# A routed two-layer block on one core: which gathers may run ahead of the last writes of X, and where two weight steps stand

## The chip, the core and the metric

The kernel runs on one core of one Trainium2 chip. The metric is the time of one execution on the device in microseconds (us); less is better. TensorE (PE) multiplies, VectorE (DVE) and ScalarE (ACT) work on what it leaves, GpSimd (POOL) issues the indexed transfers, SyncE (SP) issues most weight loads.

## The reference, cut to what matters

```python
# retention attention -> x (4608 rows of 512), then two routed layers
def _moe_ref(x, w_skip, w_gate, w1, w2):          # the first one, "A"
    do_compute = x @ w_skip > 0
    ...
    for e in range(8):                            # argmax expert of each row
        h = np.maximum(xc[mask] @ w1[e], 0.0)
        y[mask] = gate_w[mask, None] * (h @ w2[e])
    out[do_compute] = xc + y

def _moe2_ref(x, w_gate, w1, w2):                 # the second one, "B"
    logits = x @ w_gate
    cap = N // E                                  # 576 rows for each expert
    for idx in np.argsort(-logits.flatten()):     # greedy, highest logit first
        ...
    for e in range(8):
        out[mask] = np.maximum(x[mask] @ w1[e], 0.0) @ w2[e]
```

Layer B assigns rows greedily under a cap, so its experts are found one after another: expert 0's list needs all the logits, expert i+1's list needs what expert i took.

## The kernel before, in words

Every fp32 product is made as three products of a high part and a low part (H·H, H·L, L·H). A weight chunk of 512 KB is loaded into one of five raw buffers (`wraw`), ACT copies it into a high part (`w_split`, line 253), and DVE subtracts to get the low part (`w_rest`, line 187). There are four chunks of w1 and four of w2 for each expert.

Attention comes first and leaves its rows in X in DRAM. Layer A runs over eight experts of up to 352 rows each, in tiles of 128, 128 and 96: it gathers rows of X, multiplies, and scatters the changed rows back into X. Layer B runs over eight experts of 576 rows (tiles of 128, 128, 128, 128 and 64): `gather` (line 637) takes the rows by the expert's list `ids2`, `turn` transposes them on PE and leaves `xTH` and `xTL`, `layer1` writes `l1p` in two segments of columns, 0:256 and 256:576, `layer2_half` (line 737, from the raw w2) multiplies the 64 remaining rows, `layer2` (line 710) the four full tiles. For expert 0, all eight blocks f of the segment 0:256 come before those of 256:576; for the others the segments alternate block by block. The results leave through ACT and DVE (`y`) and a scatter into the output.

The rows that layer A's last expert (7) writes can belong to expert 0's list, while that list should be known early. Its rows stand in columns NT to NT+2 of the routing tables (`NC = NT + 3` columns). `first_slots` (line 1206) gives the rows of the columns from `NL` on the last slots of expert 0's list, so that the first gathers need none of them. With `NL = NT + 1`, the tiles 1 and 2 of expert 7 (224 rows) are late, and the first two gathers are free of them. `post_a` (line 1087) therefore scatters expert 7's tile 0 as soon as it is done and holds back the scatters of tiles 1 and 2 (`held_x`) until `opening` (line 1444) has issued gathers 0 and 1. Gathers 2 to 4, and the low parts of w1's chunks 0 and 1, follow after the last products of layer A. Gathers wait for every earlier scatter into X, and scatters into X wait for every earlier gather.

A planner orders the work while the program is written: `tick` adds the columns of each matmul at 2400 per us to `clock`, and every generator in `tasks` goes on when its due time (the sum of what it yields, held to no more than 0.4 behind the clock) has come. Nothing of this runs on the chip: it fixes each engine's order of instructions, and the semaphores do the rest. The generators that matter here:

- `phases` (lines 1219 to 1398) makes the lists of layer B: five rounds of counting (`cnt`, `sum`, `nfl`), then the expert's number `eix`, the prefix sums (`pfx`, `slt`), the one-hot tables (`OHh`, `MV`, `OHl`), the product `idp` (line 1340), `pt`, `idq`, and the list `ids2`. The list of expert i+1 is made while expert i is multiplied, and the phase goes on to the next expert without waiting for the pass.
- `weights_b(i)` waits until expert i+1 is known, issues the load of its first w1 chunk on SP (the number is read from `eix`), yields 3.0, copies the chunk on ACT, yields 1.5, and makes its low part on DVE; the other loads follow.
- `rows_b(i)` gathers and turns the rows of expert i+1 after its list.

For expert 0, `entry` makes the low parts of chunks 2 and 3 and turns tiles 2 to 4 during the first segment; `task(gen)[1] = clock[0] + 4.5` lets the phases go on 4.5 planner us after layer A.

Of the kernel before, what the change touches and what calls it, by code (L numbers as in the profile page):

```python
# [21 lines left out]
N, DM, FF, E = 4608, 512, 1024, 8  # L22
NT = 36
# [24 lines left out]
MAGIC = 12582912.0  # L48
HL = 33.0 * (ZOFF - 1)
NC = NT + 3  # L50
NL = NT + 1
NQ = NC + 1
NG = NQ // 4
SPLIT = 26
# [116 lines left out]
def block_kernel(ctx, tc, q_c, k_c, k_r, v_r, wg, wg2, w1a, w2a, w2t, w1b, w2b, cst, dtab, out, dbg=None):  # L171
# [14 lines left out]
    def tt(o, x, y, op):  # L186
        V.tensor_tensor(o, x, y, op)  # L187

    def ts(o, x, s1, op0, s2=None, op1=None):
        if op1 is None:  # L190
            V.tensor_scalar(o, x, s1, None, op0)
        else:
            V.tensor_scalar(o, x, s1, s2, op0, op1)  # L193

    def stt(o, x, sc, y, op0, op1):
        V.scalar_tensor_tensor(o, x, sc, y, op0, op1)  # L196
# [48 lines left out]
    def w_split(kind, c, low="pool", over=False, swap=False):  # L245
        r = wt["whole", kind, c] = wt.pop(("raw", kind, c))
        if over:
            h, l = [rawp.tile([P, 1024], F32R, name=f"ov{c}", tag="wraw") for c in "HL"]
        else:
            tag = {"w1": "w2", "w2": "w1"}[kind] if swap else kind  # L250
            h = wp.tile([P, 1024], F32R, name=f"{kind}H{c}", tag=f"{tag}H{c}")
            l = wp.tile([P, 1024], F32R, name=f"{kind}L{c}", tag=f"{tag}L{c}")
        nc.scalar.activation(h, r, AF.Copy)  # L253
        wt[kind, c] = (h, l)
        if low != "later":
            e = nc.gpsimd if low == "pool" else V
            e.tensor_tensor(l, r, h.bitcast(F32), ALU.subtract)

    def w_rest(kind, c, half=None):
        h, l = wt[kind, c]  # L260
        j = slice(0, 1024) if half is None else slice(512 * half, 512 * half + 512)
        tt(l[:, j], wt["whole", kind, c][:, j], h[:, j].bitcast(F32), ALU.subtract)
# [114 lines left out]
    with ExitStack() as actx:  # L377
# [188 lines left out]
        gen = iter(())  # L566
        for i in range(-4, NT):
# [20 lines left out]
            if i == SPLIT + 2:  # L588
                gen = route(0, SPLIT, lambda: ps_1.tile([P, 512], F32, name="qc", tag="rt1"),
                            lambda: ps_1.tile([P, 48], F32, name="idp", tag="rt1"))  # L590
# [44 lines left out]
    def gather(key, i, ids, n, tag="xg", bufs=6):  # L635
        t = xp.tile([P, DM], F32, name="xg", tag=tag, bufs=bufs)
        nc.gpsimd.indirect_dma_start(out=t[0:n, :], out_offset=None, in_=X[:, :],  # L637
                                     in_offset=bass.IndirectOffsetOnAxis(ap=ids[0:n, :], axis=0))
        xg[key, i] = t
# [102 lines left out]
    def scatter(dst, idx, src, n):  # L742
        nc.gpsimd.indirect_dma_start(out=dst[:, :], out_offset=bass.IndirectOffsetOnAxis(ap=idx, axis=0),  # L743
                                     in_=src[0:n, :], in_offset=None)
# [33 lines left out]
    def gate_dots(x2, dst, n, a, b):  # L778
        for e in range(a, b):
            j = xp.tile([P, DM], F32, name="junk", tag="junk", bufs=1)  # L780
            V.scalar_tensor_tensor(j[0:n], x2[0:n], 1.0, wgb[e // 4][0:n, e % 4], ALU.mult, ALU.mult,  # L781
                                   accum_out=dst[0:n, e:e + 1])
# [298 lines left out]
    done_a = set()  # L1081

    def release():
        while held_x:
            held_x.pop(0)()

    def post_a(e, late=False):
        def post(i, n, p):
            j = 3 * e + i
            idx = ids1[0:n, j:j + 1]  # L1090
            x2 = xp.tile([P, DM], F32, name="x2", tag="x2", bufs=4)

            def whole():
                stt(x2[0:n], p[0:n], gate[0:n, j:j + 1], xg.pop((e, i))[0:n], ALU.mult, ALU.add)

            if late:
                def job():
                    whole()
                    if e == E - 1 and i and "open" not in done_a:
                        held_x.append(lambda: scatter(X, idx, x2, n))  # L1100
                    else:
                        scatter(X, idx, x2, n)
                    if e == E - 1 and i == 0:
                        done_a.add(0)

                fill.append(job)
                return
            if e < LATE:
                whole()
            else:  # L1110
                nc.scalar.activation(x2[0:n], p[0:n], AF.Copy, scale=gate[0:n, j:j + 1])
                nc.gpsimd.tensor_tensor(x2[0:n], x2[0:n], xg.pop((e, i))[0:n], ALU.add)
            scatter(X, idx, x2, n)
            if e < LATE:
                l8 = xp.tile([P, E], F32, name="l8", tag="l8", bufs=4)
                for c in range(0, E, 2):
                    pend.append(lambda c=c: gate_dots(x2, l8, n, c, c + 2))
                pend.append(lambda: scatter(LT, idx, l8, n))
        return post
# [86 lines left out]
    def first_slots(inc, rk2, s_, b_, slt, t2):  # L1206
        a, z_ = slice(0, NL), slice(NL, NC)
        every, early, tied = inc[:, 0, NC - 1:NC], inc[:, 0, NL - 1:NL], inc[:, 1, NL - 1:NL]
        ts(slt[:, a], rk2[:, 1, a], every, ALU.add, float(CAP2), ALU.is_ge)
        stt(slt[:, a], slt[:, a], 9999.0, rk2[:, 1, a], ALU.mult, ALU.add)  # L1210
        stt(slt[:, a], slt[:, a], early, b_[:, a], ALU.add, ALU.mult)
        stt(slt[:, z_], rk2[:, 1, z_], every, b_[:, z_], ALU.add, ALU.mult)
        cb = rt("cb", [P, 1])
        ts(cb, every, tied, ALU.add, float(CAP2), ALU.min)
        tt(cb, cb, every, ALU.subtract)
        tt(t2[:, a], rk2[:, 0, a], s_[:, a], ALU.mult)
        stt(t2[:, z_], rk2[:, 0, z_], cb, s_[:, z_], ALU.add, ALU.mult)
# [169 lines left out]
    know, listed = set(), set()  # L1387
# [13 lines left out]
    clock = [0.0]  # L1401
    tasks = []

    def task(g):
        t = [g, 0.0]
        tasks.append(t)
        return t
# [13 lines left out]
    def load_b(i, eng=nc.sync):  # L1421
        r = eng.value_load(eix[0:1, i:i + 1], min_val=0, max_val=E - 1)
        return loads_dyn(r, w1b, w2b, eng=eng)

    def gathers_b(i):
        return [lambda k=k: gather(("b", i), k, ids2[:, i, k:k + 1], T2[k]) for k in range(5)]

    def late():
        yield 1.0
        gate_h(1, 0, hh, 7)  # L1430
        for d in gate_slots(1, L2[:, NT:NC, :]):
            yield d
        for d in last_claims():
            yield d
        for d in phases():
            yield d

    gen = late()

    def chain():  # L1440
        while 0 not in listed:
            yield next(gen)

    def opening():
        while 0 not in know or LATE not in done_a:
            yield 0
        for j in load_b(0)[0][0:3]:
            j()
        yield 4.0
        for c in range(3):  # L1450
            w_split("w1", c, "later", swap=True)
            yield 1.1
        while 0 not in listed or 0 not in done_a:
            if 0 in listed and fill:
                fill.pop(0)()
            yield 0
        for j in gathers_b(0)[0:2]:
            j()
        done_a.add("open")
        release()  # L1460

    first = [task(chain()), task(opening())]
    late_layers[0](tick)
    done_a.add(LATE)
# [4 lines left out]
            pass  # L1469
    while fill:  # L1470
        fill.pop(0)()
    for j in gathers_b(0)[2:5]:
        j()
    w_rest("w1", 0)
    w_rest("w1", 1)
    warm(ps1, "l1", 16)
    t0 = turns(("b", 0), T2, (2, 3))
    t0[0]()
# [25 lines left out]
            open_t.pop(0)()  # L1504

    task(entry())
    task(gen)[1] = clock[0] + 4.5

    def post_b(i):
        def post(j, n, p):  # L1510
# [12 lines left out]
    def weights_b(i):  # L1523
        if i == 0:
            yield 15.0
        if held:
            for c in (2, 3):
                w_split("w1", c, "later", swap=True)
                yield 1.2
                w_rest("w1", c)  # L1530
                if c == 2:
                    held.pop()()
                yield 1.2
        for j in halves("w2", swap=True):
            j()
            yield 2.3
        if i + 1 == E:
            return
        while i + 1 not in know:
            yield 0  # L1540
        l1, l2 = load_b(i + 1)
        l1[0]()
        yield 3.0
        w_split("w1", 0, "later", swap=True)
        yield 1.5
        w_rest("w1", 0)
        while lay[0] < 2 * i + 1 or ("tail", i) not in done:
            yield 0
        for j in l1[1:]:
            j()  # L1550
        yield 2.3
        w_split("w1", 1, "later", swap=True)
        yield 2.3
        w_rest("w1", 1)
        for j in l2[0:3]:
            j()
        held.append(l2[3])
# [63 lines left out]
```

## Time and profile before

| | |
|---|---|
| median of three runs | 969.1 us (967.52 to 969.66) |
| the profiled execution: its time, its span | 972.4 us, 970.6 us |
| mean granted TensorE clock in it | 0.981 of full speed |
| busy in the span: PE, PE weight loads, DVE, ACT, POOL | 920.3, 772.1, 652.2, 318.7, 227.7 us |
| instructions: PE, DVE | 8288, 1679 |
| DMA moved | 153.92 MB, mean 159 GB/s |
| attention, layer A, layer B (from the span's start) | 0 to 186, 186 to 477, 477 to 971 us |

The page gives each engine's busy time, the chain of work that ended last, and the costliest groups of instructions with what ended the idle time ahead of them. In the trace, a row of the timeline is one instruction, or a few alike, with its start, its length, its engine and line, what it writes and reads, and in brackets the idle time of its engine ahead of it and what ended that. `L187`, `L193` and `L196` are the lines of helpers for DVE.

### The profile page before, as it was taken

How to read it: one execution, taken by the hardware profiler on the slowest of the kernel's cores; microseconds unless marked ns; L12 is line 12 of the kernel's file. 1: busy time of each engine (PE TensorE's matmuls, PEld its weight loads, DVE VectorE, ACT ScalarE, POOL GpSimd, SP SyncE). 2: the span in 40 equal slices, each digit the busy share in tenths (PEclk: the TensorE clock that was granted, in tenths of full speed). 3: DMA queues.
4: the chain of work that ended last, by engine and by line, in shares of the span. 5: the costliest groups of instructions: out<-in, count | busy, mean ns of one | idle time of the engine just before them, and what ended most of it. 6: DMA issues, size and time to landing. Idle time of an engine off the chain costs nothing.

```text
span 970.6 us, 20470 instructions
## 1 busy us (share of the span) xinstructions
PE 920.3 (95%) x8288; PEld 772.1 (80%) x8288; DVE 652.2 (67%) x1679; ACT 318.7 (33%) x607; POOL 227.7 (23%) x205
## 2 busy tenths in 40 slices
PE   7999998699999999999989999999999999999997
PEld 7888876598888888886676887968879789697885
DVE  3566576559999999968677767757667666664230
ACT  1333433133434334341232332423324233153330
POOL 1322221203354334320210304013030030330101
PEclk7999999799999999999999999999999999999999
DMA  9899996374454456330433406144061340633201
GB/s 333 327 401 353 342 356 216 121 248 140 159 194 150 157 173 190 118 134 12 138 123 104 168 5 224 44 140 132 1 228 45 126 134 14 222 121 115 87 6 43
DMA packets 46736, 153.92 MB, mean 159 GB/s; under 512 B 7248, under 2 KB 8016, under 8 KB 46384
## 3 DMA queue, kind: packets, MB, share of 16 engines
q1 hardware_dynamic: 31824, 106.98, 32.0%
q0 software_dynamic: 10496, 30.93, 9.6%
q10 hardware_dynamic: 4320, 14.68, 3.9%
q8 instruction: 66, 1.08, 0.5%
q14 instruction: 30, 0.25, 0.1%
HBM read 127.43 MB, written 25.13 MB: 157 GB/s over the span
## 4 chain that ended last, share of the span: by engine, by line
PE 57%; DVE 16%; issue 3%; DMA 3%; ACT 1%; POOLq 0%; SPq 0%; POOL 0%; DVEq 0%; ACTq 0%
PE l1p L679 27%; PE l2p L710 23%; DVE junk L781 5%; PE trp L660 2%; DMA wraw<-in_w1b_dram 2%; DVE w2L L187 2%; DVE hL L196 1%; DVE w1L L187 1%; PE l2p L737 1%; PE cnt L1250 1%; DVE xTL L187 1%; PE idp L1340 1%; DVE x L196 1%; DVE MV L187 1%; DMA xg<-X,ids 1%
## 5 line engine op out<-in xcount | busy, mean ns | idle before, releaser
L679 PE MATMUL l1p<-xTH,w1H 128*128 128x352 f32 (+2 forms) x768 | 242.4, 316 | 4.2 <-DVE hL L196 3.0
L679 PE MATMUL l1p<-xTL,w1H 128*128 128x352 f32 (+2 forms) x768 | 234.9, 306 | 1.6 <-DVE xTL L187 1.6
L679 PE MATMUL l1p<-xTH,w1L 128*128 128x352 f32 (+2 forms) x768 | 234.1, 305 | 0.0
L710 PE MATMUL l2p<-w2H,hH 128*128 128x512 f32 (+1 forms) x448 | 186.2, 416 | 0.0
L710 PE MATMUL l2p<-w2H,hL 128*128 128x512 f32 (+1 forms) x448 | 178.2, 398 | 0.0
L710 PE MATMUL l2p<-w2L,hH 128*128 128x512 f32 (+1 forms) x448 | 178.2, 398 | 0.0
L679 PEld LDWEIGHTS l1p<-xTH,w1H 128*128 128x128 f32 x768 | 145.5, 190 | 10.1 <-DVE hL L196 5.6
L679 PEld LDWEIGHTS l1p<-xTL,w1H 128*128 128x128 f32 x768 | 145.5, 189 | 2.8 <-DVE xTL L187 2.4
L679 PEld LDWEIGHTS l1p<-xTH,w1L 128*128 128x128 f32 x768 | 145.3, 189 | 0.0
L196 DVE SCALAR_TENSOR_TENSOR hL<-l1p,hH 128x256 fp32r<-128x256 f32 (+1 forms) x192 | 85.8, 454 | 77.9 <-ACT hH L688 77.4
L688 ACT ACTIVATE hH<-l1p 128x256 fp32r<-128x256 f32 (+1 forms) x192 | 78.6, 409 | 161.5 <-PE l1p L679 158.9
L743 POOL DMA_INDIRECT out_dram<-y,ids x40 | 42.0, 1050 | 374.6 <-DVE hm L193 141.0
L781 DVE SCALAR_TENSOR_TENSOR junk<-x,wgb 128x512 f32<-128x512 f32 (+1 forms) x144 | 99.0, 688 | 3.1
L710 PEld LDWEIGHTS l2p<-w2H,hL 128*128 128x128 f32 (+1 forms) x448 | 83.2, 186 | 21.7 <-issue 0.2
L710 PEld LDWEIGHTS l2p<-w2H,hH 128*128 128x128 f32 (+1 forms) x448 | 83.5, 186 | 18.8 <-issue 1.6
L710 PEld LDWEIGHTS l2p<-w2L,hH 128*128 128x128 f32 (+1 forms) x448 | 83.6, 187 | 16.9
L637 POOL DMA_INDIRECT xg<-X,ids x64 | 75.6, 1181 | 65.5 <-issue 28.7
L253 ACT ACTIVATE w1H<-wraw 128x1024 fp32r<-128x1024 f32 x64 | 65.4, 1056 | 70.8 <-DMA wraw<-in_w1b_dram 65.8
L661 ACT ACTIVATE xTH<-trp 128x512 fp32r<-128x512 f32 (+2 forms) x64 | 35.5, 558 | 124.9 <-PE trp L660 123.9
L187 DVE TENSOR_TENSOR w1L<-wraw,w1H 128x1024 fp32r<-128x1024 f32 x60 | 71.6, 1217 | 2.9 <-ACT w1H L253 2.5
L187 DVE TENSOR_TENSOR w2L<-wraw,w2H 128x1024 fp32r<-128x1024 f32 (+1 forms) x61 | 73.0, 1197 | 0.0
L253 ACT ACTIVATE w2H<-wraw 128x1024 fp32r<-128x1024 f32 x64 | 67.4, 1055 | 12.7 <-PE l2p L710 7.3
(263 smaller groups left out, 1127.4 us busy)
## 6 DMA issues: line engine op xcount, KB each, us to landing
wraw<-in_w2a_dram SPq DMA_DIRECT2D x31, 512.0 KB, 4.7
wraw<-in_w1b_dram SPq DMA_DIRECT2D x31, 512.0 KB, 4.6
wraw<-in_w1a_dram SPq DMA_DIRECT2D x28, 512.0 KB, 4.4
wraw<-in_w2b_dram SPq DMA_DIRECT2D x28, 512.0 KB, 4.2
X<-xo ACTq DMA_DIRECT2D x16, 512.0 KB, 6.7
kU<-in_k_c_dram SPq DMA_DIRECT2D x15, 512.0 KB, 9.1
qU<-in_q_c_dram SPq DMA_DIRECT2D x15, 512.0 KB, 7.7
vU<-in_v_r_dram SPq DMA_DIRECT2D x15, 512.0 KB, 8.4
```

What stands on the lines that cost most here:

```text
L187: V.tensor_tensor(o, x, y, op)
L196: V.scalar_tensor_tensor(o, x, sc, y, op0, op1)
L253: nc.scalar.activation(h, r, AF.Copy)
L637: nc.gpsimd.indirect_dma_start(out=t[0:n, :], out_offset=None, in_=X[:, :], in_offset=bass.IndirectOffsetOnAxis(ap=ids[0:n, :], axis=0))
L660: nc.tensor.transpose(p[:, k, 0:n], g[0:n, k * P:(k + 1) * P], ident[0:n, 0:n])
L661: nc.scalar.activation(h[:, :, off:off + n], p[:, :, 0:n], AF.Copy)
L679: nc.tensor.matmul(o, lhsT=wx[:, c:c + P], rhs=xx[:, k, a:b], start=(n == 0), stop=(n == 11))
L688: nc.scalar.activation(hh[0][:, f, a:b], o, AF.Relu)
L710: nc.tensor.matmul(p[0:n, :], lhsT=x[:, f, off:off + n], rhs=y[:, c:c + 512], start=(f == 0 and j == 0), stop=(f == 7 and j == 2))
L737: nc.tensor.matmul(p[64 * h:64 * h + 64, :], lhsT=ht[:, g], rhs=w[g // 2][:, c:c + 512], start=(f == 0), stop=(f == 3), tile_position=(0, ...
L743: nc.gpsimd.indirect_dma_start(out=dst[:, :], out_offset=bass.IndirectOffsetOnAxis(ap=idx, axis=0), in_=src[0:n, :], in_offset=None)
L781: V.scalar_tensor_tensor(j[0:n], x2[0:n], 1.0, wgb[e // 4][0:n, e % 4], ALU.mult, ALU.mult, accum_out=dst[0:n, e:e + 1])
```

## The change

Two columns instead of one are early (`NL = NT + 2`): only the 96 rows of expert 7's last tile take late slots. Expert 7's tile 1 is scattered as soon as it is done, tile 2 alone may be held, and `opening` waits for tile 1's job instead of tile 0's. Three gathers instead of two are then issued there, and the low parts of w1's chunks 0 and 1 are placed right behind them, no longer behind the last gathers. The phases go on 1.0 instead of 4.5 planner us after layer A. In `weights_b`, the planner time from the load of the next expert's first w1 chunk to its copy on ACT is 5.5 instead of 3.0.

```diff
-NL = NT + 1
+NL = NT + 2
@@ post_a
-                    if e == E - 1 and i and "open" not in done_a:
+                    if e == E - 1 and i == 2 and "open" not in done_a:
                         held_x.append(lambda: scatter(X, idx, x2, n))
                     else:
                         scatter(X, idx, x2, n)
-                    if e == E - 1 and i == 0:
-                        done_a.add(0)
+                    if e == E - 1 and i == 1:
+                        done_a.add(1)
@@ opening
-        while 0 not in listed or 0 not in done_a:
+        while 0 not in listed or 1 not in done_a:
             if 0 in listed and fill:
                 fill.pop(0)()
             yield 0
-        for j in gathers_b(0)[0:2]:
+        for j in gathers_b(0)[0:3]:
             j()
         done_a.add("open")
         release()
+        w_rest("w1", 0)
+        w_rest("w1", 1)
@@ after layer A
-    for j in gathers_b(0)[2:5]:
+    for j in gathers_b(0)[3:5]:
         j()
-    w_rest("w1", 0)
-    w_rest("w1", 1)
@@
-    task(gen)[1] = clock[0] + 4.5
+    task(gen)[1] = clock[0] + 1.0
@@ weights_b
         l1[0]()
-        yield 3.0
+        yield 5.5
         w_split("w1", 0, "later", swap=True)
```

## Rows read from the trace of the kernel before

**Rows 1.** PE's waits from 477 to 960 us: total, times, longest

```profile
PE idp L1340 <- DVE OHl L187: 12.1, 6, 2.3
```

**Rows 2.** Timeline of PE in pass 0, the list of expert 1

```profile
532.81 0.92 PE L1340 MATMUL idp<-MV,OHl 128*128 128x160 bf16 x10 [1.62 <-DVE OHl L187]
```

**Rows 3.** Timeline of pass 1 around the list of expert 2, engine by engine

```profile
577.73 0.18 PE L1262 MATMUL nfl<-fl,ones 128*128 128x8 bf16 x1
577.84 3.65 PE L737 MATMUL l2p<-wraw,hT 128*64 128x512 f32 x16
...
590.10 0.92 PE L1340 MATMUL idp<-MV,OHl 128*128 128x160 bf16 x10 [2.06 <-DVE OHl L187]
...
580.79 2.23 SPq L242 DMA_DIRECT2D wraw<-in_w1b_dram  x4
...
584.24 1.06 ACT L253 ACTIVATE w1H<-wraw 128x1024 fp32r<-128x1024 f32 x1 [5.82 <-DMA wraw<-in_w1b_dram]
585.20 0.57 ACT L1512 ACTIVATE y<-l2p 64x512 f32<-64x512 f32 x1
...
585.81 0.69 DVE L187 TENSOR_TENSOR y<-l2p,y 64x512 f32<-64x512 f32 x1 [2.75 <-ACT y L1512]
...
587.45 1.22 DVE L187 TENSOR_TENSOR w1L<-wraw,w1H 128x1024 fp32r<-128x1024 f32 x1
...
589.55 0.89 DVE L187 TENSOR_TENSOR OHl<-hl,kq 128x640 bf16<-128x640 bf16 x2
```

**Rows 4.** Windows, passes 1 and 2: length, five engines' busy (count), clock, DMA share, GB/s

```profile
549.60:610.30 60.70, 58.63 (x430) 49.16 (x429) 41.87 (x128) 20.11 (x42) 11.24 (x10) 1.00 0.33 109
610.30:672.40 62.10, 60.04 (x431) 49.96 (x429) 41.35 (x126) 20.31 (x42) 10.91 (x10) 0.97 0.32 107
```

**Rows 5.** Windows, columns of rows 4: one us of pass 2, three us after its stall

```profile
653.00:654.00 1.00, 1.00 (x4) 0.66 (x2) 0.36 (x1) 0.00 (x0) 1.00 (x1) 0.50 0.02 8
```

**Rows 6.** Timeline of PE in the opening of layer B

```profile
479.69 0.66 PE L660 MATMUL trp<-cs,xg 128*128 128x128 f32 x4 [0.64 <-DMA xg<-X,ids]
...
481.76 0.38 PE L679 MATMUL l1p<-xTL,w1H 128*128 128x256 f32 x1 [0.34 <-DVE xTL L187]
...
495.64 0.66 PE L660 MATMUL trp<-cs,xg 128*128 128x128 f32 x4 [2.05 <-DMA xg<-X,ids]
...
499.06 0.42 PE L679 MATMUL l1p<-xTL,w1H 128*128 128x320 f32 x1
...
503.24 0.41 PE L1250 MATMUL cnt<-OH,M 128*128 128x32 bf16 x10 [0.54 <-DVE M L187]
```

**Rows 7.** Timeline of POOL: scatters into X and gathers around the opening

```profile
456.46 0.99 POOL L743 DMA_INDIRECT X<-x,ids  x1 [21.25 <-DVE part L1252]
459.98 0.92 POOL L743 DMA_INDIRECT X<-x,ids  x1 [2.53 <-DVE fl L187]
...
476.00 0.97 POOL L637 DMA_INDIRECT xg<-X,ids  x1 [0.30 <-issue]
479.91 1.32 POOL L743 DMA_INDIRECT X<-x,ids  x1 [2.94 <-DMA xg<-X,ids]
484.61 1.51 POOL L743 DMA_INDIRECT X<-x,ids  x1 [3.38 <-DVE hL L196]
488.69 0.98 POOL L637 DMA_INDIRECT xg<-X,ids  x1 [2.58 <-issue]
```

**Rows 8.** Chain of waits: two blocks of layer 1 back to back (start, length)

```profile
617.50 3.27 PE l1p L679 x24
```

**Rows 9.** Timeline of DVE: tiles 1 and 2 of expert 7

```profile
471.72 0.75 DVE L196 SCALAR_TENSOR_TENSOR x<-l2p,gate,xg 128x512 f32<-128x512 f32 x1
...
477.36 0.75 DVE L196 SCALAR_TENSOR_TENSOR x<-l2p,gate,xg 96x512 f32<-96x512 f32 x1 [3.43 <-PE l2p L710]
```

**Rows 10.** Windows, columns of rows 4: the opening's first segment, and the counting after it

```profile
481.70:498.92 17.22, 13.47 (x109) 12.75 (x109) 11.30 (x41) 5.11 (x11) 4.37 (x4) 1.00 0.26 82
498.92:503.10 4.18, 3.78 (x25) 3.38 (x24) 3.97 (x11) 1.25 (x5) 0.00 (x0) 1.00 0.90 318
```

## The prediction, made before the changed kernel was run

> **What bounds the kernel now.** I read the page first: PE is busy for 95% of the span, so only idle PE and slow PE can be won. The waits of PE from the opening of layer B on come next: one line holds most of it, PE's list product `idp` waiting for DVE's one-hot table `OHl`, six times, 12.1 us [rows 1]. That is once in each of the passes 0 to 5 while the next expert's list is made: 1.62 in pass 0 [rows 2], about 2.1 in each of the passes 1 to 5, for which pass 1 stands.
>
> The timeline of pass 1 tells why [rows 3]. Call the start of the half product H (577.84). The last count matmul (`nfl`) stands just ahead of it, so the expert's number is known late and SP issues the load of its first w1 chunk at H+2.95. ACT's copy waits 5.82 us for that load, until H+6.40. The partial sum of the 64 rows stands behind the copy on ACT and gets out at H+7.36, though its product ended at H+3.65. DVE waits 2.75 us for it, and behind it come the rest of the list's tables and the low part of that chunk (1.22): `OHl` begins at H+11.7, and PE has stood still for 2.06 us. So a load that is asked for late and a copy that waits for it ahead of other work hold ACT, then DVE, then PE.
>
> The windows show a second price [rows 4]: pass 2 does the work of pass 1 in 62.1 instead of 60.7 us. Inside it the granted clock falls to 0.50 (1.2 GHz) after the stall [rows 5]. Passes 3 and 5 look like pass 2, pass 4 like pass 1: three falls, 1.4 us each.
>
> Last, the opening of layer B: there PE waits on gathers, 2.05 us in one place [rows 6], and the indexed transfers on X wait for one another [rows 7].
>
> **The change part by part.**
>
> *The copy and the phases.* They belong together. I add up the planner's yields by hand, before and after. The phases begin 3.5 planner us earlier and keep a lead of 2.8 to 3.5 through the passes 1 to 5. `nfl` and the number's load then stand 24 matmuls of layer 1 ahead of the half product, 3.3 us [rows 8]: the load is issued at H−0.3 instead of H+2.95. Its raw buffer is free (five tiles back is w1's chunk 3 of the running expert, split early in the pass), and SP has nothing else ahead of it. The copy, due 5.5 after the load, comes in the half product's third quarter: still ahead of the partial sum on ACT. But it now starts at about H+3.2 (load to copy took 3.45 [rows 3]) and ends at H+4.2, when the partial sum has been ready for only 0.6. That gets out at H+4.7, DVE adds it at H+4.8. On DVE the tables up to the first `MV` stand ahead of it; behind it come the second `MV` (0.5), the low part (1.1) and `OHl`: these begin at H+7.0, and `idp` can follow 0.55 later, the gap in [rows 3]: H+7.5. The planner puts `idp` 12 matmuls earlier than before, so PE has run dry at H+7.3 (before: 590.10 less 2.06, H+10.2; 27 matmuls from H+3.65 give 0.24 each). Left is 0.2 to 0.3 us of the 2.06: a gain of 1.8 in each of five passes, **9.0**. Bounds: 2.1 each if nothing is left (10.5); 1.3 each if the load takes half a us longer, or DVE is late by that (6.5).
>
> In pass 0 the copy comes after `idp` altogether; DVE has only the list's own tables, one low part of w2 (1.2) and the add of the partial sum ahead of it. I get `OHl` 0.2 after PE is ready: **1.4** of 1.62, bounds 1.0 and 1.6.
>
> *The clock.* With no stall of 2 us, the three falls should go: 3 × 1.4 = **4.2** in the profiled execution. Two executions need not have the same falls: passes 1 and 4 had the stall and no fall. For the median I take 1.4 to 4.2, middle 2.8.
>
> *The scatter of tile 1 ahead of the gathers.* This costs. Its x2 is made at 471.72 to 472.46 [rows 9], ahead of the list, so its scatter starts at 472.7. The gathers must now wait for its landing. From one transfer's start to that of the next dependent one the rows show 3.52 (456.46 to 459.98, a quiet moment), 4.70 and 4.08 [rows 7]; I take 4.1. So gather 0 starts at 476.8, and gather 1 at 478.1 instead of 476.00. The first layer-1 products start as much later, since they wait for tile 1's turn [rows 6]: **2.1 late** (1.5 to 2.7). The Trainium skill (DMA: Bandwidth & Descriptors, Anatomy of one DMA — SWDGE (gpsimd) path) gives such a transfer about 2.0 us and its bytes at 436 GB/s, an estimate of 2.6 us for 256 KB; by it gather 0 would start at 475.3 and the opening would be 1.5 better. The traces show none under 3.52 here.
>
> *Three gathers ahead, the low parts earlier.* Gather 2 goes out at about 479.4 instead of 488.69, gathers 3 and 4 behind the last scatter at about 487.5: none is waited for, and the 2.05 and the smaller wait ahead of it go. The two low parts (2.35 us) fill DVE's 3.43 us ahead of tile 2 [rows 9] and cost nothing there; they run while POOL waits for a landing.
>
> *What is late next.* DVE. Between the first full product (481.76) and the first product of the second segment (499.06 [rows 6]) lie 17.3 us, with 11.3 of DVE work [rows 10]. The earlier phases bring in the next expert's claims and first mask as well, nearly all of the 4.0 us that follow [rows 10], and the planner puts them ahead of the `xTL` of tile 4 that the second segment needs. That makes 15 of work, and about 16 with the gaps and DVE's wait for `cct`; the bank that each layer-1 block needs is freed by DVE behind this work. So the segment takes 16 instead of 17.3: 1.3 gained, not the 4 that PE alone would allow. After it, a wait of 0.54 for the first count [rows 6] is gone, and 0.15 of small matmuls come in. Opening: 2.1 − 1.3 − 0.4 = **0.4 slower**, from −0.5 to 1.2. And between 478 and 484 PE does little but turn two tiles: a fall of the clock, 1.4, is somewhat more likely than not there. With 0.9 for it, the opening costs **1.3** (−0.5 to 3.0).
>
> *The late slots* themselves change two columns instead of one in three small DVE instructions: nothing.
>
> **Sum.** 9.0 + 1.4 − 1.3 = 9.1 of stalls, and 2.8 of clock (4.2 in the profiled execution): 11.9. Against the profiled execution's own 972.4, with 4.2: 13.3, 959.1. The median, 969.1, is 3.3 below that execution, by the profiling or by two falls fewer; so from it I take 11.9: **957.2 us**.
>
> **The rivals.**
>
> 1. *The copy still holds DVE.* For it: it stays ahead of the partial sum, and `idp` comes earlier as well. Against: the load gains 3.3 us, the place of `idp` 2.9. If the chunk lands 1 us later than I take it, `OHl` does as well, half of each stall stays (5 lost) and the clock still falls (2.8 lost): 965.0.
> 2. *Slower: the load doesn't move.* Its mechanism is the load's start. If something besides the expert's number holds it to the half product (a raw buffer that this product still reads), the chunk lands no earlier against PE, the stall of 2.06 comes back whole at the new, earlier place, and the opening's price (1.3 to 3.0, and the 1.6 of pass 0 not won) is all that is left: 970.4 to 972.1. It decides from a landing later than H+5. Against it: by the order of the five raw buffers that chunk's is free long before, and SP has nothing else to wait for than the number.
> 3. *The gathers don't wait.* If the scatter lands within 2.6 us and DVE keeps up, the opening gains 3 instead of costing 1.3: 953.
> 4. *It doesn't do what it says.* The three gathers are issued ahead of X's last write, but wait for the last but one. That is in the forecast; alone it would leave the loop as forecast.
>
> **How the numbers follow.** Forecast 0.76 (952.5 to 962), rival 1 0.12, rival 2 0.07, rival 3 0.05. The range 952.0 to 963.5 runs from all stalls gone with three falls won and an opening that gains 0.5 (17 us) to 1.3 in each pass, one fall won and the opening at 3.0 (about 6 us); it leaves out rival 2 and most of rival 1. A measurement here tells about 0.2%, 2 us. Faster by more: forecast, rivals 1 and 3, less a little: 0.91. Within: the low end of rival 2: 0.04. Slower: 0.05.
>
> **What would show it.** In passes 1 to 5, the load's start against the half product (H−0.3), ACT's copy without a wait of 5.8, `idp` with an idle time under 0.5, and passes of about 58.5 us with a clock of 1.00. In the opening, a gather 0 that waits for a scatter until 476.8, no waits for gathers after tile 1, layer-1 blocks waiting for DVE, and a second segment that starts at 499 to 501. I would be wrong if the copy still waits long for its load, or if another engine's wait of 2 us stands in front of `idp`, `pfx` or the turns.

## The result, and the profile after

| | before | after |
|---|---|---|
| median | 969.4 us (967.5 to 975.5) | 958.5 us (956.5 to 960.5) |
| ratio after/before, 95% interval | | 0.988 (0.983 to 0.993) |
| the same on another chip, beside experiments | 970.0 us | 958.5 us, 0.9885 (0.986 to 0.991) |
| profiled execution: time, span, mean granted clock | 972.4, 970.6 us, 0.981 | 956.5, 954.8 us, 0.986 |

The median falls by 10.9 us, 1.1%, with an interval clear of 1; 957.2 was forecast. The waits of PE from 470 to 960 us come first (total, times, longest). The line of [rows 1] is gone, and the gathers and a count are what is left:

```profile
PE trp L660 <- DMA xg<-X,ids: 2.9, 2, 2.3
PE cnt L1250 <- DVE M L187: 2.2, 2, 1.2
```

Pass 1 again, engine by engine (start, length, engine, line, what it writes and reads, idle time ahead); these lines answer [rows 3]. H, the half product's start, is 576.17 here.

```profile
576.17 1.08 PE L737 MATMUL l2p<-wraw,hT 128*64 128x512 f32 x4
...
583.69 0.52 PE L1340 MATMUL idp<-MV,OHl 128*128 128x160 bf16 x5
...
575.86 4.65 SPq L242 DMA_DIRECT2D wraw<-in_w1b_dram  x4
...
579.15 1.06 ACT L253 ACTIVATE w1H<-wraw 128x1024 fp32r<-128x1024 f32 x1 [2.38 <-DMA wraw<-in_w1b_dram]
580.23 0.59 ACT L1512 ACTIVATE y<-l2p 64x512 f32<-64x512 f32 x1
...
580.85 0.69 DVE L187 TENSOR_TENSOR y<-l2p,y 64x512 f32<-64x512 f32 x1 [0.26 <-ACT y L1512]
...
581.95 1.22 DVE L187 TENSOR_TENSOR w1L<-wraw,w1H 128x1024 fp32r<-128x1024 f32 x1
583.08 0.88 DVE L187 TENSOR_TENSOR OHl<-hl,kq 128x640 bf16<-128x640 bf16 x2
```

The load starts at H−0.31, the copy at H+2.98, the table at H+6.91, and `idp` follows at H+7.52 with no idle time. ACT's order is the one of [rows 3]: the copy still stands directly ahead of the partial sum (579.15, then 580.23). The windows from one half product to the next, passes 1 and 2 (columns of [rows 4], which they answer), show equal lengths, PE busy throughout, and the clock at 1.00:

```profile
576.17:634.89 58.72, 58.72 (x429) 48.82 (x428) 41.41 (x125) 20.54 (x42) 12.51 (x10) 1.00 0.32 113
634.89:693.62 58.73, 58.73 (x429) 48.80 (x428) 41.39 (x125) 20.44 (x42) 12.49 (x10) 1.00 0.33 113
```

The opening of layer B has paid for this. First PE (answers [rows 6]), then POOL (answers [rows 7]), DVE around the x of tile 2 (answers [rows 9]), and two windows (columns of [rows 4]):

```profile
477.98 0.66 PE L660 MATMUL trp<-cs,xg 128*128 128x128 f32 x4 [2.29 <-DMA xg<-X,ids]
...
479.43 0.66 PE L660 MATMUL trp<-cs,xg 128*128 128x128 f32 x4 [0.57 <-DMA xg<-X,ids]
...
481.49 0.58 PE L679 MATMUL l1p<-xTL,w1H 128*128 128x256 f32 x1 [0.34 <-DVE xTL L187]
...
498.20 0.41 PE L1250 MATMUL cnt<-OH,M 128*128 128x32 bf16 x10 [1.19 <-DVE M L187]
498.47 0.39 PE L679 MATMUL l1p<-xTH,w1H 128*128 128x320 f32 x1
```

```profile
470.90 0.96 POOL L743 DMA_INDIRECT X<-x,ids  x1 [5.90 <-DVE pt L1343]
474.58 1.00 POOL L637 DMA_INDIRECT xg<-X,ids  x1 [2.72 <-DMA X<-x,ids]
475.88 0.98 POOL L637 DMA_INDIRECT xg<-X,ids  x1 [0.30 <-PE idle L232]
477.17 0.95 POOL L637 DMA_INDIRECT xg<-X,ids  x1 [0.31 <-issue]
481.72 0.93 POOL L743 DMA_INDIRECT X<-x,ids  x1 [3.61 <-DVE zd L1359]
```

```profile
471.37 2.36 DVE L187 TENSOR_TENSOR w1L<-wraw,w1H 128x1024 fp32r<-128x1024 f32 x2
474.81 0.74 DVE L196 SCALAR_TENSOR_TENSOR x<-l2p,gate,xg 96x512 f32<-96x512 f32 x1 [1.08 <-PE l2p L710]
```

```profile
479.00:482.00 3.00, 1.55 (x7) 1.11 (x8) 1.84 (x7) 0.86 (x2) 0.28 (x1) 0.84 0.76 210
482.00:485.00 3.00, 3.00 (x18) 3.00 (x17) 1.89 (x5) 0.39 (x1) 0.66 (x1) 0.59 0.36 117
```

Gather 0 starts 3.68 us after the start of tile 1's scatter; PE waits 2.29 for it, and some 3 us behind that wait the granted clock falls to the lower level (0.50 of full speed, 1.2 GHz) for some 3 us.

To see where the time went I cut both profiled executions at three marks: the start of the idle matmuls behind layer A's last product (16 matmuls whose results nobody uses, only there to keep PE working; 477.16 before, 474.62 after), the half product of pass 0, and that of pass 7.

| us | before | after | gained |
|---|---|---|---|
| up to the end of layer A (the work is the same) | 477.16 | 474.62 | 2.54 |
| opening: to pass 0's half product | 39.06 | 41.05 | −1.99 |
| loop: from pass 0's half product to pass 7's | 421.93 | 406.62 | 15.31 |

Behind the last half product both take 26.3 us to their last matmul. The 2.54 cannot be told from chance: layer A ends anywhere from 473.0 to 479.6 us in the profiled executions of all the kernels here, with and without the opening's edits. Nor is the opening's 1.99 the last word: the second profiled execution of the changed kernel has 43.70 there, 4.64 more than before, with a loop of 406.54.

### The profile page after: what moved, and what is told of

Same layout as the page of the kernel before. It is cut to its first block, busy times and chain, and to the rows that moved or that the text cites. A ratio compares the mean times of both kernels' runs of the same rounds, so it can differ in the third digit from the quotient of the medians.

```text
span 954.8 us, 20461 instructions
## 1 busy us (share of the span) xinstructions
PE 917.4 (96%) x8288; PEld 768.0 (80%) x8288; DVE 652.7 (68%) x1679; ACT 319.9 (34%) x607; POOL 234.4 (25%) x205
## 3 DMA queue, kind: packets, MB, share of 16 engines
q8 instruction: 66, 1.08, 0.4%
## 4 chain that ended last, share of the span: by engine, by line
PE 63%; DVE 14%; issue 2%; ACT 1%; DMA 1%; POOLq 0%; DVEq 0%; ACTq 0%
PE l1p L679 28%; PE l2p L710 26%; DVE junk L781 5%; PE l2p L737 3%; PE trp L660 2%; DVE w2L L187 2%; DVE hL L196 1%; DVE xTL L187 1%; PE cnt L1250 1%; DVE x L196 1%; DVE w1L L187 1%; PE idp L1340 1%; ACT xTH L661 0%; PE sum L1258 0%; DMA xg<-X,ids 0%
## 5 line engine op out<-in xcount | busy, mean ns | idle before, releaser
L743 POOL DMA_INDIRECT out_dram<-y,ids x40 | 45.2, 1130 | 351.8 <-DVE y L187 179.1
L637 POOL DMA_INDIRECT xg<-X,ids x64 | 80.6, 1259 | 64.4 <-DMA X<-x,ids 19.9
```

## The experiments

**The theory** before the first of them: the loop's two edits bring the whole gain, the opening's edits cost about 2 us. **The rivals**: the opening carries part of the gain; and, on how the loop gains, the prediction's own account (the load's start, 3.3 us earlier, is what counts) against another (the place of the copy on ACT decides).

The change has three parts: opening (slots, scatter, gathers, low parts), phases (4.5 to 1.0), copy (3.0 to 5.5). The first runs make some of them alone.

**Copy alone.**

```diff
         l1[0]()
-        yield 3.0
+        yield 5.5
         w_split("w1", 0, "later", swap=True)
```

> Only the copy later (5.5 instead of 3.0 after the load); phases and opening as before, so the load is still issued 2.95 us after the start H of the half product. Theory (the copy's place decides): the partial sum of the 64 rows gets out at H+3.7 instead of H+7.4, the copy at H+6.4 to H+7.4, its low part to H+8.7 and the one-hot table to H+9.6; PE runs dry at H+10.2, so nearly nothing of the 2.06 is left in passes 1 to 5, and the clock's falls go: 956 to 960, with no earlier load at all. Rival (the load's start decides): the chunk lands as late as before, its low part still holds the table, 1.3 to 2 us of each stall stay: 965 to 970.

Measured: 954.0 us, ratio 0.9855 (0.981 to 0.990). The rival falls. The timeline of pass 1 of this kernel, with H at 573.16 (SP, ACT, DVE, PE):

```profile
576.11 2.23 SPq L242 DMA_DIRECT2D wraw<-in_w1b_dram  x4
...
576.88 0.59 ACT L1512 ACTIVATE y<-l2p 64x512 f32<-64x512 f32 x1 [3.14 <-PE l2p L737]
579.46 1.06 ACT L253 ACTIVATE w1H<-wraw 128x1024 fp32r<-128x1024 f32 x1 [1.98 <-DVE hl L193]
...
578.41 0.69 DVE L187 TENSOR_TENSOR y<-l2p,y 64x512 f32<-64x512 f32 x1
...
581.14 1.22 DVE L187 TENSOR_TENSOR w1L<-wraw,w1H 128x1024 fp32r<-128x1024 f32 x1
582.27 0.89 DVE L187 TENSOR_TENSOR OHl<-hl,kq 128x640 bf16<-128x640 bf16 x2
...
583.20 0.87 PE L1340 MATMUL idp<-MV,OHl 128*128 128x160 bf16 x10
```

The load is issued at H+2.95 and the copy starts at H+6.30, both as in the kernel before (H+2.95, H+6.40 [rows 3]). What has moved is the partial sum, from H+7.36 to H+3.72. DVE no longer waits for it, the table begins at H+9.11 instead of H+11.71, and PE's idle time is gone. With the copy behind the partial sum, the late load holds nothing up.

**Phases alone.**

```diff
-    task(gen)[1] = clock[0] + 4.5
+    task(gen)[1] = clock[0] + 1.0
```

> Only the phases earlier (1.0 instead of 4.5 after layer A); the copy stays 3.0 after the load. Theory (the copy's place decides): the load is issued some 3.3 us earlier, but the copy then stands 3.3 us earlier on ACT too, ahead of layer 1's last eviction; ACT waits for the load there and PE stands still in the half product or ahead of the list's product for about 1.5 to 2 us in each pass: 966 to 971. Rival (the load's start decides, as the prediction's sum has it: 3.3 us earlier against the half product): most of the stall goes, 957 to 961.

Measured: 973.8 us, 1.0062 (1.004 to 1.009): slower. ACT, DVE and PE in pass 1 (H 572.20):

```profile
575.19 1.06 ACT L253 ACTIVATE w1H<-wraw 128x1024 fp32r<-128x1024 f32 x1 [4.25 <-DMA wraw<-in_w1b_dram]
576.15 0.21 ACT L685 ACTIVATE hT<-l1p 128x64 f32<-128x64 f32 x1
576.25 0.38 ACT L688 ACTIVATE hH<-l1p 128x256 fp32r<-128x256 f32 x1
577.52 0.59 ACT L1512 ACTIVATE y<-l2p 64x512 f32<-64x512 f32 x1 [0.89 <-PE l2p L737]
...
576.66 0.42 DVE L196 SCALAR_TENSOR_TENSOR hL<-l1p,hH 128x256 fp32r<-128x256 f32 x1 [4.94 <-ACT hH L688]
...
583.11 0.92 PE L1340 MATMUL idp<-MV,OHl 128*128 128x160 bf16 x10 [1.93 <-DVE OHl L187]
```

The load comes 3.3 us earlier, as forecast, but the copy is tied to the load: it moves too, now ahead of layer 1's last eviction (`hT`, `hH`), and holds ACT for 4.25 us there. DVE waits 4.94 us for `hH`, with the list's tables behind that. The half product waits for `hT` and takes 5.2 us from its first matmul to the first full product (3.66 in the run above), and the stall of 1.93 stays.

**The order, with 0.2 between the two.** By the planner's sums the copy stands ahead of the partial sum up to 3.8 and behind it from 4.0 on.

```diff
-        yield 3.0
+        yield 3.8      # the other kernel: 4.0
```

> The kernel before with the copy 3.8 instead of 3.0 after the load: by the planner's sums the copy then still stands ahead of the partial sum of the 64 rows on ACT, by one place; with 4.0 it stands behind it. Theory (the order of these two on ACT is all): the stalls of some 2 us ahead of the list's product stay in passes 1 to 5, 967 to 972. Rival (the distance itself counts, the chunk having more time to land): four fifths of the gain is there already, 955 to 959.

> The kernel before with one number changed: the copy 4.0 instead of 3.0 after the load, the least with which the copy comes behind the partial sum of the 64 rows on ACT (right behind it); phases and opening as before. Theory (this one place decides): 953 to 957, as with 5.5. Rival (it takes the larger distance, so that the chunk has landed before the copy's turn): ACT waits for the chunk behind the partial sum and holds its next evictions; 960 to 966.

Measured: with 3.8, 969.4 us, 0.9994 (0.997 to 1.001); with 4.0, 953.6 us, 0.9833 (0.981 to 0.985), each against the kernel before on its own chip. ACT in pass 1, first with 3.8 (H 575.91), then with 4.0 (H 572.62):

```profile
582.23 1.06 ACT L253 ACTIVATE w1H<-wraw 128x1024 fp32r<-128x1024 f32 x1 [5.73 <-DMA wraw<-in_w1b_dram]
583.19 0.57 ACT L1512 ACTIVATE y<-l2p 64x512 f32<-64x512 f32 x1
```

```profile
576.34 0.59 ACT L1512 ACTIVATE y<-l2p 64x512 f32<-64x512 f32 x1 [3.14 <-PE l2p L737]
578.94 1.06 ACT L253 ACTIVATE w1H<-wraw 128x1024 fp32r<-128x1024 f32 x1 [2.01 <-DVE hl L193]
```

The same two instructions, in the other order. The copy starts at H+6.32 in both, 3.36 and 3.37 us after the issue of its load; the partial sum leaves 3.6 us earlier in the second, and 16 us of the whole follow. PE's waits for `OHl` are 11.9 us, six times, in the first; 0.3 us, once, in the second. It is the order, not the distance. In the two traces the matmuls, the instructions of ACT and DVE and the transfers stand in the same order but for six swaps: this one, once in each of the passes 1 to 5, and one on DVE in pass 0, where the second `MV` table stands behind the chunk's low part with 3.8 and ahead of it with 4.0 (stalls of 2.07 and 0.33).

This does not make the load's start worthless. In the changed kernel the order on ACT is still that of 3.8, copy ahead of partial sum, and the load 3.3 us earlier has taken the stall away. There are two ways out: the partial sum ahead of the copy, or the copy ahead of it with a chunk that lands early. The phases alone are neither, since the copy moves ahead of `hT` with its load.

**The opening alone, and the loop's two edits alone.** The diffs are those of the change, the first without its last two edits, the second with nothing but these.

> The opening's edits alone (late slots for 96 rows, tile 1's scatter ahead, three gathers, low parts); phases 4.5 after layer A and copy 3.0 after the load, as in the kernel before. Theory: all six stalls ahead of the list's product stay (12 us), gather 0 still waits some 3.7 us from the scatter's start, and the opening moves by -1 to +2: 968.5 to 971.5 where the kernel before has 969.4. Rival: the opening's edits carry part of the gain: 964 to 967.

> The loop's two edits alone (phases 1.0 instead of 4.5 after layer A, copy 5.5 instead of 3.0 after the load); slots, scatters, gathers and low parts of the opening as in the kernel before. Theory: the opening's edits cost about 2 us and the loop's two bring the whole gain, so this is faster than the changed kernel by 1 to 3 us: 955.5 to 957.5 where the changed one has 958.5 and the one before 969.4. Rival: the three gathers ahead of X's last write save the wait of 2.05 and pay for themselves; then this is 959 to 961, slower than the changed kernel.

Measured: the opening alone 974.0 us, 1.0052 (1.003 to 1.008), even slower than I expected; its opening takes 41.49 us, 2.4 more than before, and the stalls stay (11.1 us in passes 0 to 5). The loop alone: 957.0 us, 0.9874 (0.984 to 0.991), hardly better than the whole change and 3 us behind the copy alone. So beside the later copy the phases cost as well.

**The change without one of the loop's edits.** Without the phases, then without the copy:

```diff
-    task(gen)[1] = clock[0] + 1.0
+    task(gen)[1] = clock[0] + 4.5
```

> The changed kernel without the earlier phases (4.5 after layer A as before); opening and later copy as changed. Theory: no wait ahead of the list's product in passes 1 to 5, but the opening still pays for gather 0's wait for the scatter (2.3 us, and a fall of the clock behind it): 956 to 960, against some 954 for the copy alone. Rival (the price comes from the earlier phases, by DVE's work and the count's wait of 1.2 us): 953 to 955.

```diff
-        yield 5.5
+        yield 3.0
```

> The changed kernel without the later copy (3.0 after the load as before); opening and earlier phases as changed. Theory: the copy stands ahead of layer 1's last eviction and holds ACT, PE waits some 1.9 us ahead of the list's product in passes 1 to 5, and the opening's price comes on top: 973 to 980, slower than the kernel before. Rival (the earlier load carries the gain, and the place of the copy is only a refinement): 957 to 962.

Measured: 956.3 us, 0.9873 (0.985 to 0.990), and 976.8 us, 1.0093 (1.006 to 1.013). With these all eight combinations have been run:

| copy | phases | opening | ratio | us, opening and loop of the profiled execution |
|---|---|---|---|---|
| | | | 1 | 39.06, 421.93 |
| x | | | 0.9855 (4.0: 0.9833) | 37.49, 407.00 (4.0: 38.46, 405.25) |
| | x | | 1.0062 | 37.43, 426.31 |
| | | x | 1.0052 | 41.49, 420.73 |
| x | x | | 0.9874 | 40.49, 406.88 |
| x | | x | 0.9873 | 41.21, 406.49 |
| | x | x | 1.0093 | 40.94, 425.88 |
| x | x | x | 0.9877, 0.9885 | 41.05, 406.62; 43.70, 406.54 |

The copy gains 14 to 21 us whatever the others are. The other two never gain. Alone each costs some 5 or 6 us, beside the copy 2 to 4 by the medians (the intervals are wider than that); the last of the three adds nothing that can be told.

**What the opening pays for.** Two kernels beside the changed one on the same chip. One holds tile 1's scatter back too:

```diff
-                    if e == E - 1 and i == 2 and "open" not in done_a:
+                    if e == E - 1 and i and "open" not in done_a:
```

The other fills PE's wait with idle matmuls:

```diff
-    warm(ps1, "l1", 16)
+    warm(ps1, "l1", 48)
...
-    warm(ps1, "l1", 4)
+    warm(ps1, "l1", 12)
```

> The changed kernel once more, beside the next three on one chip: 957 to 960. Its loop of layer B (first to last half product) should again show no wait ahead of the list's product and passes of 58.7 us; its opening should again show the granted clock at 0.50 for some 3 us after the wait of 2.3 us for gather 0.

> The changed kernel with the scatter of expert 7's tile 1 held back as well until the three gathers are issued, so that these wait only for the scatter of tile 0. Rows of tile 1 that are in the first three tiles of expert 0's list are then read before they are written: that part of the computation is changed, and the time tells only what the gathers' wait for the scatter costs. Theory: gather 0 starts some 3.5 us earlier, PE's wait of 2.3 us for it goes, and with it the clock's fall; DVE's work in the segment gives part back: 2 to 4 us faster than the changed kernel beside it. Rival: DVE sets the end of the opening, the first product comes earlier and the second segment does not: less than 1 us.

> The changed kernel with more idle matmuls ahead of tile 0's turn (48 instead of 16, some 3.2 us instead of 1.07) and between the turns of tiles 0 and 1 (12 instead of 4), so that PE works through its wait for gather 0; nothing else is changed. Theory (the opening's price has a part that is clock): the granted clock stays at 1.00 in the opening, the first segment's 1.7 us at half clock come back, and this is 1 to 2 us faster than the changed kernel beside it. Rival (the opening's price is the wait itself, and DVE sets the segment's length whatever PE's clock): no difference, within 0.5 us.

Measured: the changed kernel 958.5 us, 0.9885 (0.986 to 0.991); held 953.6, 0.9838 (0.982 to 0.986); filled 957.5, 0.9871 (0.985 to 0.989). By the medians the gathers' wait for the scatter costs 4.9 us, the falls of the clock behind it included; 2 to 4 were expected. POOL and PE of the held kernel (idle matmuls end layer A at 473.85 there), then a window of the changed kernel in this set and one of the kernel with the filled wait, 3 us in about the same place of the opening:

```profile
471.39 1.25 POOL L637 DMA_INDIRECT xg<-X,ids  x1 [7.15 <-DVE ids L196]
...
475.05 0.66 PE L660 MATMUL trp<-cs,xg 128*128 128x128 f32 x4
...
476.56 0.66 PE L660 MATMUL trp<-cs,xg 128*128 128x128 f32 x4 [0.63 <-DMA xg<-X,ids]
```

```profile
480.00:483.00 3.00, 2.86 (x14) 2.83 (x14) 2.13 (x10) 0.08 (x1) 0.93 (x1) 0.50 0.50 175
```

```profile
483.00:486.00 3.00, 3.00 (x28) 3.00 (x27) 2.90 (x7) 0.86 (x3) 0.64 (x1) 1.00 0.36 111
```

Held: gather 0 goes out as soon as the list is there, PE no longer waits for it (2.44 in the changed kernel of this set), only 0.63 for gather 1, and the clock stays up. Filled: twice as many matmuls in 3 us. From the first full product to the second segment it takes 15.63 us, against 17.89 for the changed kernel in this set (16.98 in its first profile); its fall lasts some 7 us here, some 3 there. So the fall is real, and in the one profiled execution of the filled kernel it is absent. What it is worth is not decided: the medians differ by 1.0, the intervals overlap, and the runs of either kernel spread over 3 us or more. One reason is that the clock can fall a second time, behind the count's wait of 1.19 us; it did so in the profiled executions of both kernels of this set (the changed one's window), and not in the first profile of the changed kernel:

```profile
498.00:501.00 3.00, 3.00 (x23) 2.57 (x20) 1.20 (x6) 0.33 (x1) 0.00 (x0) 0.64 0.89 317
```

**A faster version.** The kernel before with the copy at 4.0 beats both (953.6 us, 0.9833; the changed kernel beside it 0.9885). I tried to better the copy alone by phases a little earlier, since in its passes 1 and 4 a turn waits 0.56 and 1.10 us for a late gather:

```diff
-    task(gen)[1] = clock[0] + 4.5
+    task(gen)[1] = clock[0] + 2.0
...
-        yield 3.0
+        yield 5.5
```

> The kernel before with the copy 5.5 after the load and the phases 2.0 (not 4.5, not 1.0) after layer A, for a faster kernel than both: the list's product then stands 3 matmuls earlier in a pass than with 4.5, 0.7 us. Theory: no wait ahead of the list's product, the waits for late gathers in the passes (0.2 to 1.7 us in all with 4.5) go, the opening stays as before: 952 to 955. Rival: the earlier phases already bring DVE's work into the opening and a longer wait for the first count, with a fall of the clock: 956 to 958.

Measured: 957.8 us, 0.9886 (0.986 to 0.992): the rival. The profiled execution, at 963.0 us the slowest of the six, shows that DVE's added work holds the second segment up at its second product (PE's row), and that a fall of the clock follows, 0.71 from 501 to 504 us:

```profile
501.66 0.41 PE L679 MATMUL l1p<-xTL,w1H 128*128 128x320 f32 x1 [1.73 <-DVE xTL L187]
```

The wait for a late gather stayed too (1.06 in pass 4). So the version with one number changed stands.

## Why the prediction was right, and where it was not

**The loop's size: right.** 9.0 + 1.4 + 4.2 = 14.6 were forecast for the profiled execution, 15.3 measured. The lines of the six stalls went whole where 0.2 to 0.3 each was to be left, but the passes are shorter by a little less than the stalls: 1.87 and 1.73 us in the passes 1 and 4 (1.8 forecast), 3.3 to 3.8 in those that had a fall (3.2), 1.12 in pass 0 (1.4). The windows show the clock at 1.00. The working of pass 1 held to a few tenths: load H−0.3 (H−0.31), copy from H+3.2 (2.98), partial sum out at H+4.7 (4.65, the end of its eviction; the H+7.36 for the kernel before is a start), added from H+4.8 (4.68), table from H+7.0 (6.91), `idp` at H+7.5 (7.52). Passes took 58.72 us (forecast 58.5).

**The loop's cause: right for this kernel, wrong about what it takes.** I took the gain from the load's earlier start, with a later copy that keeps its place on ACT. That is what the changed kernel does: its copy stands ahead of the partial sum as in [rows 3], and the load is issued at H−0.31. The step that failed is "They belong together". The later copy does without the earlier phases: alone it goes behind the partial sum, and the stalls are gone with the load as late as before. The phases do not do without the copy, alone they lose. The list needs nothing of that chunk; it needs DVE, and DVE needed the partial sum that stood behind the copy. I priced only the sum of both edits, so I did not see the shorter way; the profile of the changed kernel confirms my working line by line and could not have shown it either. Rival 2's point, "a landing later than H+5", was never put to the test: in the run with the copy alone the copy starts at H+6.3 and nothing stalls, but there it stands behind the partial sum.

The Trainium skill (PSUM — Partial Sum Buffer, Engine vs sequencer instructions) calls the queue of ScalarE strict FIFO; the runs with 3.8 and 4.0 agree, a ready instruction of 0.57 us having stood 3.6 us longer behind one that waited for its data.

**The opening: direction right, price low.** Forecast 1.3 slower; 1.99 in the first profiled execution, 4.64 in the second, and 2 to 4 us beside the copy by the medians. The forecast's terms are 2.1 for the first product, −1.3 for the segment, −0.4 for what follows, and 0.9 for the clock; the first profile has 2.27, −0.11 with the clock in it, and −0.17. One by one:

- Scatter to gather: 4.1 taken, 3.68 measured, but the scatter starts 0.7 later than I had it (470.90, against 472.7 less the 2.54 of layer A). First full product 2.27 late, 2.1 forecast. The Trainium skill (DMA: Bandwidth & Descriptors, Anatomy of one DMA — SWDGE (gpsimd) path), by which I estimated 2.6 us for such a transfer, falls 1.1 short of the 3.68 from one start to that of the transfer that depends on it. The trace doesn't show where the difference lies.
- Low parts in DVE's idle time: right, 3.43 [rows 9] became 1.08.
- DVE the bound of the segment: 16 forecast; 15.63 without a fall (filled), 16.98 and 17.89 with one. The 17.3 of the kernel before run to the second product of the second segment (499.06); to the first, as counted here, it is 17.09, so less was there to gain.
- The first count: wrong. I had its wait of 0.54 gone; instead a count waits 1.19 us for its mask at the segment's end (0.54, as before, in the changed kernel without the earlier phases: they bring the count forward more than its mask). What follows to pass 0's half product gained 0.17 (17.20 instead of 17.37) where 0.4 was forecast.
- The fall of the clock: weighed at 0.9 as somewhat likelier than not. It comes in each of the five profiled executions in which PE waits 2.2 us or more for gather 0, for some 3 us in two and some 7 in three, and behind the count's wait there is sometimes a second.

**The sum.** 11.9 were forecast for the median, 10.9 measured. It is partly luck that these are so close: two terms were off in opposite directions. The loop gave 0.7 more than forecast, the opening took 0.7 more in the first profile and 3.3 more in the second.

**The rivals.** 1 (the copy still holds DVE) and 2 did not come. 3 (the gathers don't wait) priced the opening without the wait at 953; the held kernel has 953.6. The waits of the gathers for the scatter are real, as rival 4 has it, and the three gathers are never waited for after tile 1.

**Still open:** why the opening's edits cost 5 us or more alone. The profiled execution shows 2.4 more in the opening than the kernel before, and 1.2 less in the loop. But the old opening, with the phases as before, takes 37.49 to 39.06 us in four profiled executions, and that of the kernel before is the longest of them, so the price there is 2.4 to 4.0. The rest may lie in how often and how long the clock falls, which one profile cannot tell. For the phases alone the loop explains it (4.4 more). Beside the copy, they have 3.0 more in the opening (40.49 against 37.49), with two falls of the clock there; alone 37.43 and no fall.

## What to carry to other kernels

Ahead of an instruction that waits for a transfer, look at what stands behind it on its engine and who waits for that: putting the ready one first was worth 16 us here by itself. Starting the transfer earlier lost 5 us by itself and helped only where the copy kept its place. Where one number ties two instructions together (a load and its copy), moving the first moves the second, and an earlier load can make things worse. Price each edit of a combined change alone as well as in the sum, since a right total does not show which edits it needs, and edits that only cost can hide behind one that gains.

## What the runs showed of the hardware that I had not expected

- Where PE waited 2.2 to 2.5 us for gather 0, the granted clock fell to 0.50 (1.2 GHz) 2 to 4 us behind in 5 of 5 profiled executions. Where it waited for gather 0 not at all, or 0.44 us with more idle matmuls, and at most 0.67 for gather 1, it fell there in 1 of 9. With 2.85 us of idle matmuls instead of 1.07 in that place it stayed at 1.00 (2.4 GHz) until the count's wait.
- The spread of one kernel goes with the clock: twelve executions of the kernel with the opening alone went from 969.0 us at a mean granted clock of 0.987 to 978.3 us at 0.973.
- The stalls of some 2 us in the loop were about equal in all passes, but the falls behind them (0.97 in the window of a pass) were not in all: passes 2, 3 and 5 in the kernel before and in that with the opening alone; 0, 2, 4 and 5 with the copy at 3.8; 1 and 3 with the phases alone; 1 and 2 in the change without the later copy. Nothing here tells which of them the clock follows.
